# Pooling attention followed by a GELU MLP: K and V of a batch in one 128-partition tile, attention in full-array matmuls, and the remainder group second to last

## The chip, the cores and the metric

The kernel runs on one core of a Trainium2 chip. The metric is the device time of one execution in microseconds (us); each kernel was run four times or more, and medians are quoted. For each run the profile also gives the span (first to last instruction, some 2 us less than the timed value of the same run) and the mean clock that TensorE was granted, as a share of full speed.

The engines are called as in the profile: PE is TensorE, ACT is ScalarE, DVE is VectorE, POOL is GpSimd; SP issues DMAs, and "SPq" or "ACTq" lines are issues of DMAs by SP or ACT.

## The reference

```python
# q, k, v: (8 batches, 8 heads, 576 tokens, 64); w_in: 512 x 2048; w_out: 2048 x 512; all float32
def _attn_ref(q, k, v):
    ...
    k_p = k.reshape(B, H, Sp, pool, D).mean(axis=3)      # pool = 8, Sp = 72
    v_p = v.reshape(B, H, Sp, pool, D).mean(axis=3)
    scores = scale * np.matmul(q, k_p.transpose(0, 1, 3, 2))
    ...                                                   # softmax over the 72 pooled keys
    return np.matmul(attn, v_p)

def _moe_ref(x, w_in, w_out):                             # x: 4608 tokens x 512
    h = x @ w_in
    g = 0.5 * h * (1.0 + np.tanh(c * (h + 0.044715 * h * h * h)))
    return g @ w_out
```

The two matrix products of the MLP are nearly all of the work. Tokens are handled in nine groups of 512: groups 0 to 7 are the first 512 tokens of each batch, and the remainder group holds the last 64 tokens of all eight.

## The kernel before

Its main loop runs the MLP of one group and hangs pieces of the next group's attention into it at numbered steps. Steps 0 to 63 are the matmuls with W_in (64 of 128x512), steps 64 to 127 those with W_out. The MLP of one group, with what is hung into it, is called a stage below.

```python
    def scores(g, pr):                       # pr is a pair of heads
        ...
            for hh in range(2):
                p0 = 64 * hh                 # half of the array for each head
                nc.tensor.matmul(out=sc[:, hh, :], lhsT=kpT[p0:p0 + 64, g, pr, :],
                                 rhs=qT[p0:p0 + 64, pr, :], start=True, stop=True)
        ...
        nc.scalar.activation(out=e, in_=sc, func=ACT.Exp, scale=1.0 / 64.0)

    def attend(g, pr):
        ...                                  # den: sums of e, o: values, two half-array matmuls each
        nc.scalar.activation(out=lden, in_=den, func=ACT.Ln)
        nc.scalar.activation(out=r, in_=lden, func=ACT.Exp, scale=-1.0)
        ...
            nc.vector.tensor_tensor(out=xo, in0=o, in1=r, op=ALU.mult)
    ...
            p0, dp = (104, 6) if late else (64, 14)      # late: group 1, during group 0's MLP
            for pr in range(HP):
                at(p0 + dp * pr, scores, n, pr)
                at(p0 + dp * pr + dp // 2, attend, n, pr)
```

1/denominator is taken as exp(-ln(denominator)), so that exp and ln share one activation table; gelu needs another: in ACT's timeline in the prediction, exp, ln and exp (e, lden, r) follow each other without a table load, and one of 1.28 us stands between gelu and e. K and V are loaded with 72 partitions each and pooled by DVE in four trees a batch.

The softmax here doesn't subtract the row's maximum and nothing guards it: scores larger than these inputs give would overflow.

Of the kernel before, what the change touches and what calls it, by code (L numbers as in the profile page):

```python
# [8 lines left out]
F32 = mybir.dt.float32  # L9
BF16 = mybir.dt.bfloat16  # L10
# [7 lines left out]
def kernel(  # L18
# [12 lines left out]

    nc = tc.nc
# [6 lines left out]
    NG = B + 1  # L39
    MAIN = 512  # L40
    HP = H // 2

    consts = ctx.enter_context(tc.tile_pool(name="consts", bufs=1))
    wst = ctx.enter_context(tc.tile_pool(name="wst", bufs=2))
    kvp = ctx.enter_context(tc.tile_pool(name="kvp", bufs=6))
# [6 lines left out]
    kpT = consts.tile([128, B, HP, Sp], BF16, name="kpT")  # L52
    vs = consts.tile([Sp, B, H, D], BF16, name="vs")
    identb = consts.tile([128, 128], BF16, name="identb")
    ones8 = consts.tile([Sp, 64], BF16, name="ones8")

    st = [dict() for _ in range(NG)]


    def load_k(b, parts, eng):  # L60
        n = H // parts
        st[b]["k"] = []
        for i in range(parts):
            t = kvp.tile([Sp, n, 8, D], F32, name="kv")
            eng.dma_start(out=t, in_=k[b, i * n:(i + 1) * n].rearrange("h (sp pl) d -> sp h pl d", pl=8))
            st[b]["k"].append(t)

    def load_v(b, parts, eng):
        n = H // parts
        st[b]["v"] = []  # L70
        for i in range(parts):
            t = kvp.tile([Sp, n, 8, D], F32, name="kv")
            eng.dma_start(out=t, in_=v[b, i * n:(i + 1) * n].rearrange("h (sp pl) d -> sp h pl d", pl=8))
            st[b]["v"].append(t)

    def load_q(g, eng):
        t = work.tile([128, H, 4, D], F32, name="q_sb")
        st[g]["q"] = t
        if g < B:
            eng.dma_start(out=t, in_=q[g, :, :MAIN, :].rearrange("h (p j) d -> p h j d", j=4))  # L80
        else:
            for b in range(B):
                eng.dma_start(out=t[16 * b:16 * b + 16],
                              in_=q[b, :, MAIN:, :].rearrange("h (p j) d -> p h j d", j=4))


    def cast_q(g, js, eng):
        if "qb" not in st[g]:
            st[g]["qb"] = work.tile([128, 4, H, D], BF16, name="q_b")
        o = st[g]["qb"][:, js[0]:js[-1] + 1]  # L90
        i = st[g]["q"][:, :, js[0]:js[-1] + 1, :].rearrange("p h j d -> p j h d")
        if eng is nc.scalar:
            eng.copy(out=o, in_=i)
        else:
            eng.tensor_copy(out=o, in_=i)  # L95

    def pool8(t, res):
        nc.vector.tensor_tensor(out=t[:, :, 0:4, :], in0=t[:, :, 0:4, :], in1=t[:, :, 4:8, :], op=ALU.add)  # L98
        nc.vector.tensor_tensor(out=t[:, :, 0:2, :], in0=t[:, :, 0:2, :], in1=t[:, :, 2:4, :], op=ALU.add)  # L99
        nc.vector.tensor_tensor(out=res, in0=t[:, :, 0, :], in1=t[:, :, 1, :], op=ALU.add)  # L100

    def pool_k(b, i):
        if "kp" not in st[b]:
            st[b]["kp"] = work.tile([Sp, H, D], BF16, name="kp")
        t = st[b]["k"][i]
        n = t.shape[1]
        pool8(t, st[b]["kp"][:, i * n:(i + 1) * n, :])

    def pool_v(b, i):
        t = st[b]["v"][i]  # L110
        n = t.shape[1]
        pool8(t, vs[:, b, i * n:(i + 1) * n, :])

    def k_transpose(b, prs, eng):
        tp = psum.tile([128, HP, Sp], BF16, name="mm", tag="mm", bufs=4)
        for pr in prs:
            nc.tensor.transpose(out=tp[:, pr, :], in_=st[b]["kp"][:, 2 * pr:2 * pr + 2, :],  # L117
                                identity=identb[:Sp, :Sp])
        lo, hi = prs[0], prs[-1] + 1
        if eng is nc.scalar:  # L120
            eng.copy(out=kpT[:, b, lo:hi, :], in_=tp[:, lo:hi, :])
        else:
            eng.tensor_copy(out=kpT[:, b, lo:hi, :], in_=tp[:, lo:hi, :])  # L123

    def q_transpose(g, half):
        if "qT" not in st[g]:
            st[g]["qT"] = work.tile([128, HP, MAIN], BF16, name="qT")
        tp = psum.tile([128, 2, 4, 128], BF16, name="mm", tag="mm", bufs=4)
        for i in range(2):
            pr = 2 * half + i  # L130
            for j in range(4):
                nc.tensor.transpose(out=tp[:, i, j, :], in_=st[g]["qb"][:, j, 2 * pr:2 * pr + 2, :],  # L132
                                    identity=identb)
        nc.vector.tensor_copy(out=st[g]["qT"][:, 2 * half:2 * half + 2, :],  # L134
                              in_=tp.rearrange("p i j t -> p i (j t)"))

    def scores(g, pr):
        sc = psum.tile([Sp, 2, MAIN], F32, name="sc", bufs=1)
        qT = st[g]["qT"]
        if g < B:  # L140
            for hh in range(2):
                p0 = 64 * hh
                nc.tensor.matmul(out=sc[:, hh, :], lhsT=kpT[p0:p0 + 64, g, pr, :],  # L143
                                 rhs=qT[p0:p0 + 64, pr, :], start=True, stop=True)
        else:
            for b in range(B):
                for hh in range(2):
                    p0 = 64 * hh
                    nc.tensor.matmul(
                        out=sc[:, hh, 64 * b:64 * b + 64].rearrange("s (j p) -> s j p", j=4),  # L150
                        lhsT=kpT[p0:p0 + 64, b, pr, :],
                        rhs=qT[p0:p0 + 64, pr, :].rearrange("d (j b p) -> d b j p", j=4, b=B)[:, b],
                        start=True, stop=True)
# [4 lines left out]
    def attend(g, pr):  # L158
        e = st[g][("e", pr)]
        o = psum.tile([128, MAIN], F32, name="o", bufs=1)  # L160
        den = psum.tile([128, MAIN], F32, name="den", bufs=1)
        for hh in range(2):
            p0 = 64 * hh
            nc.tensor.matmul(out=den[p0:p0 + 64, :], lhsT=ones8, rhs=e[:, hh, :], start=True, stop=True)  # L164
        if g < B:
            for hh in range(2):
                p0 = 64 * hh
                nc.tensor.matmul(out=o[p0:p0 + 64, :], lhsT=vs[:, g, 2 * pr + hh, :],  # L168
                                 rhs=e[:, hh, :], start=True, stop=True)
        else:  # L170
            for b in range(B):
                for hh in range(2):
                    p0 = 64 * hh
                    nc.tensor.matmul(out=o[p0:p0 + 64, 64 * b:64 * b + 64], lhsT=vs[:, b, 2 * pr + hh, :],
                                     rhs=e[:, hh, 64 * b:64 * b + 64], start=True, stop=True)
        lden = work.tile([128, MAIN], F32, name="lden")
        nc.scalar.activation(out=lden, in_=den, func=ACT.Ln)  # L177
        r = work.tile([128, MAIN], F32, name="r")
        nc.scalar.activation(out=r, in_=lden, func=ACT.Exp, scale=-1.0)  # L179
# [3 lines left out]
        if g < B:  # L183
            nc.vector.tensor_tensor(out=xo, in0=o, in1=r, op=ALU.mult)  # L184
        else:
            nc.vector.tensor_tensor(out=xo.rearrange("d (j b p) -> d b j p", j=4, b=B),
                                    in0=o.rearrange("d (b j p) -> d b j p", j=4, b=B),
                                    in1=r.rearrange("d (b j p) -> d b j p", j=4, b=B), op=ALU.mult)


    def w_in_chunk(c):
        t = wst.tile([128, KO, 512], F32, name="wst")
        nc.sync.dma_start(out=t, in_=moe_w_in[:, 512 * c:512 * c + 512].rearrange("(ko p) f -> p ko f", p=128))
        return t

    def w_out_chunk(c):
        t = wst.tile([128, 4, DM], F32, name="wst")
        nc.sync.dma_start(out=t, in_=moe_w_out[512 * c:512 * c + 512, :].rearrange("(fo p) c -> p fo c", p=128))
        return t
# [11 lines left out]
    def mlp(g, hooks, pair_r):  # L211
# [11 lines left out]
        nc.scalar.preload_act_table_set(EXP_SET)  # L223
        nr = 2 if pair_r else 1
# [13 lines left out]
        for s in sorted(hooks):  # L238
            hook(s)
# [4 lines left out]
    load_k(0, 4, nc.sync)  # L244
    load_q(0, nc.scalar)
    nc.scalar.preload_act_table_set(EXP_SET)
    load_v(0, 2, nc.sync)
    make_identity(nc, identb)
    nc.gpsimd.memset(ones8, 8.0)
    wi = [w_in_chunk(0), w_in_chunk(1)]  # L250

    def cast_w(dst, t, eng, lo, hi):
        eng.tensor_copy(out=dst[:, lo:hi], in_=t[:, lo:hi])  # L253

    for pr in range(4):
        pool_k(0, pr)
        k_transpose(0, [pr], nc.scalar)
    cast_q(0, [0, 1], nc.scalar)
    cast_q(0, [2, 3], nc.gpsimd)
    q_transpose(0, 0)  # L260
    q_transpose(0, 1)
    pool_v(0, 0)
    pool_v(0, 1)
    scores(0, 0)
    for c in range(4):
        dst = w_in_b[:, :, 512 * c:512 * c + 512]
        if c < 3:
            scores(0, c + 1)
        attend(0, c)
        cast_w(dst, wi[c], nc.vector, 0, 2)  # L270
        cast_w(dst, wi[c], nc.gpsimd, 2, 4)
        if c < 2:
            wi.append(w_in_chunk(c + 2))
# [71 lines left out]
```

## Time and profile before

| | before |
|---|---|
| time, median (lowest to highest) | 356.21 us of 3 runs (353.85 to 356.89) |
| span of the profiled run, mean clock | 356.7 us, 0.983 (this run took 358.48 us, more than the three timed ones) |
| a middle stage | 34.2 us, of which PE 33.1 busy |
| group 0 until group 1's MLP | 79.6 us (its start, corrected for a short wait) |
| after the last W_out matmul | about 8 us, only stores |

The lines behind it are shown and read in the prediction. In a line of the timeline, the first number is the start, the second the time of the whole run of equal instructions (x7: seven), and brackets hold the idle time of the engine just before and what ended it. In a stretch view, each engine's busy us is followed by the number of its instructions; the last three columns are granted clock, DMA share and GB/s.

### The profile page before, as it was taken

Reading aid. Unit: us, or ns where it says so; the run is one execution under the profiler, and the core shown is the slowest. Engines: PE = TensorE matmul, PEld = TensorE weight load, DVE = VectorE, ACT = ScalarE, POOL = GpSimd, SP = SyncE. Lnnn points to the kernel's source line nnn. Section 1 sums busy time; section 2 is a strip of 40 time slices with the busy share of each in tenths; the row PEclk is TensorE's granted clock in tenths of the full one; section 3 lists DMA queues with packets and bytes.
Section 4 is the critical chain, followed back from the end, with each engine's and each line's share of the span. In section 5 each row is a group of like instructions: output and inputs, shape, how many; then the busy total and the mean of one; then the engine's idle time right before and its main releaser. Section 6 shows DMA issues by size and latency. Waiting matters only on the chain.

```text
span 356.7 us, 4161 instructions
## 1 busy us (share of the span) xinstructions
PE 309.4 (87%) x1656; PEld 132.1 (37%) x1656; DVE 141.5 (40%) x203; ACT 192.6 (54%) x276; POOL 30.9 (9%) x24
## 2 busy tenths in 40 slices
PE   0357974789899989998999899989988999899990
PEld 0212432224334533453345334433533354444440
DVE  2693133529333913590367137613861320230010
ACT  1265730286755675567556756675556657656500
POOL 0133432020200020002000200010020000000000
PEclk9999998899999999999999999999999999999997
DMA  7938999838701861185139314941610100010022
GB/s 236 250 136 324 290 349 230 230 106 211 229 33 59 231 182 59 60 238 146 59 99 255 89 62 125 237 111 59 125 24 29 59 31 0 31 61 29 2 58 60
DMA packets 28970, 46.40 MB, mean 130 GB/s; under 512 B 1816, under 2 KB 11032, under 8 KB 28952
## 3 DMA queue, kind: packets, MB, share of 16 engines
q1 hardware_dynamic: 27912, 45.10, 44.0%
q10 hardware_dynamic: 1040, 1.05, 1.0%
q8 instruction: 13, 0.21, 0.3%
q14 instruction: 5, 0.04, 0.0%
HBM read 36.70 MB, written 9.44 MB: 129 GB/s over the span
## 4 chain that ended last, share of the span: by engine, by line
PE 66%; DVE 12%; DMA 10%; ACT 8%; issue 1%; POOL 1%; SPq 0%; DVEq 0%
PE mm L232 30%; PE mm L220 26%; DMA kv<-in_v_dram 4%; DVE kv L98 4%; PE den L164 3%; ACT e L155 3%; DVE kv L99 3%; ACT L223 3%; DMA kv<-in_k_dram 2%; PE sc L143 2%; DMA wst<-in_moe_w_in_dram 2%; PE o L168 2%; PE mm L132 2%; DMA wst<-in_moe_w_out_dram 2%; DVE vs L100 1%; ACT gT L222 1%
## 5 line engine op out<-in xcount | busy, mean ns | idle before, releaser
L232 PE MATMUL mm<-w_out_b,gT 128*128 128x512 bf16 x576 | 138.4, 384 | 2.1 <-POOL w_out_b L253 2.0
L220 PE MATMUL mm<-xT,w_in_b 128*128 128x512 bf16 x576 | 131.4, 383 | 2.6 <-DVE xT L184 1.2
L222 ACT ACTIVATE gT<-mm 128x512 bf16<-128x512 f32 x144 | 86.0, 597 | 60.3 <-PE mm L220 60.2
L220 PEld LDWEIGHTS <-w_in_b 128*128 128x128 bf16 x576 | 55.7, 99 | 68.2 <-issue 6.6
L232 PEld LDWEIGHTS <-gT 128*128 128x128 bf16 x576 | 51.3, 98 | 74.0 <-issue 22.2
L155 ACT ACTIVATE e<-sc 72x1024 bf16<-72x1024 f32 x36 | 36.7, 1019 | 45.4 <-PE sc L143 42.2
L184 DVE TENSOR_TENSOR xT<-o,r 128x512 bf16<-128x512 f32 x32 | 22.1, 691 | 89.4 <-ACT r L179 82.4
L98 DVE TENSOR_TENSOR kv<-kv 72x1024 f32<-72x1024 f32 (+1 forms) x34 | 39.2, 1152 | 27.3 <-DMA kv<-in_k_dram 17.7
L236 DVE COPY osb<-mm 128x512 f32<-128x512 f32 x36 | 24.7, 690 | 60.4 <-PE mm L232 60.4
L177 ACT ACTIVATE lden<-den 128x512 f32<-128x512 f32 x36 | 21.4, 596 | 25.3 <-PE den L164 25.2
L95 POOL CAST q_b<-q_sb 128x2048 bf16<-128x2048 f32 (+1 forms) x9 | 16.4, 1818 | 203.7 <-DMA q_sb<-in_q_dram 142.7
L99 DVE TENSOR_TENSOR kv<-kv 72x512 f32<-72x512 f32 (+1 forms) x34 | 23.7, 698 | 1.2
L164 PE MATMUL den<-e,ones 72*64 72x512 bf16 x72 | 15.7, 428 | 9.1 <-ACT e L155 8.5
L179 ACT ACTIVATE r<-lden 128x512 f32<-128x512 f32 x36 | 22.7, 630 | 1.1
L132 PE MATMUL mm<-identb,q_b 128*128 128x128 bf16 x144 | 12.4, 238 | 6.2 <-POOL q_b L95 4.9
L168 PE MATMUL o<-e,vs 72*64 72x512 bf16 x64 | 13.8, 417 | 3.6 <-DVE xT L184 3.4
L143 PE MATMUL sc<-qT,kpT 64*72 64x512 bf16 x64 | 14.2, 439 | 3.0 <-DVE kpT L123 1.9
L134 DVE COPY qT<-mm 128x1024 bf16<-128x1024 bf16 x18 | 11.7, 681 | 8.3 <-PE mm L132 8.3
L132 PEld LDWEIGHTS <-q_b 128*128 128x128 bf16 x144 | 10.7, 108 | 10.6 <-POOL q_b L95 5.4
L164 PEld LDWEIGHTS <-ones 72*64 72x64 bf16 x72 | 5.3, 109 | 24.2 <-issue 24.1
L117 PE MATMUL mm<-identb,kp 72*128 72x72 bf16 x32 | 3.0, 201 | 12.7 <-DVE kp L100 12.7
L222 ACT ACT_TABLE_LOAD x9 | 11.5, 1283 | 0.2
(25 smaller groups left out, 70.4 us busy)
## 6 DMA issues: line engine op xcount, KB each, us to landing
kv<-in_v_dram SPq DMA_DIRECT2D x16, 576.0 KB
out_dram<-osb SPq DMA_DIRECT2D x32, 256.0 KB
kv<-in_k_dram SPq DMA_DIRECT2D x14, 576.0 KB
q_sb<-in_q_dram SPq DMA_DIRECT2D x7, 1024.0 KB
wst<-in_moe_w_in_dram SPq DMA_DIRECT2D x4, 1024.0 KB
wst<-in_moe_w_out_dram SPq DMA_DIRECT2D x4, 1024.0 KB
kv<-in_k_dram SPq DMA_DIRECT2D x4, 288.0 KB
q_sb<-in_q_dram ACTq DMA_DIRECT2D x1, 1024.0 KB
```

Of the source, the lines that this page charges most:

```text
L98: nc.vector.tensor_tensor(out=t[:, :, 0:4, :], in0=t[:, :, 0:4, :], in1=t[:, :, 4:8, :], op=ALU.add)
L99: nc.vector.tensor_tensor(out=t[:, :, 0:2, :], in0=t[:, :, 0:2, :], in1=t[:, :, 2:4, :], op=ALU.add)
L132: nc.tensor.transpose(out=tp[:, i, j, :], in_=st[g]["qb"][:, j, 2 * pr:2 * pr + 2, :], identity=identb)
L155: nc.scalar.activation(out=e, in_=sc, func=ACT.Exp, scale=1.0 / 64.0)
L164: nc.tensor.matmul(out=den[p0:p0 + 64, :], lhsT=ones8, rhs=e[:, hh, :], start=True, stop=True)
L177: nc.scalar.activation(out=lden, in_=den, func=ACT.Ln)
L179: nc.scalar.activation(out=r, in_=lden, func=ACT.Exp, scale=-1.0)
L184: nc.vector.tensor_tensor(out=xo, in0=o, in1=r, op=ALU.mult)
L220: nc.tensor.matmul(out=hp, lhsT=w_in_b[:, ko, fo * 128:(fo + 1) * 128], rhs=xT[:, ko, :], start=(ko == 0), stop=(ko == KO - 1))
L222: nc.scalar.activation(out=gT[:, fo, :], in_=hp, func=ACT.Gelu_apprx_tanh)
L232: nc.tensor.matmul(out=ops[i], lhsT=gT[:, fo, (r0 + i) * 128:(r0 + i + 1) * 128], rhs=w_out_b[:, fo, :], start=(fo == 0), stop=(fo == FO - 1))
L236: nc.vector.tensor_copy(out=osb, in_=ops[i])
```

## The change

The intent is to make PE's work whole. K and V of a batch share one tile of 128 partitions (64 each), so that one pooling tree does both; pooled V is moved into place by DMA. K is padded with zeros so that scores use the full array, and the values' tile holds 64 columns of 8.0 beside the 64 of V, so that one matmul for each head gives values in partitions 0 to 63 and sums in 64 to 127. The remainder group, whose stores are small, is handled before the last batch. The core of the diff:

```diff
+    R = B
+    seq = list(range(B - 1)) + [R, B - 1]
...
+    kpT = consts.tile([128, B, H, Sp], BF16, name="kpT")
+    vx = consts.tile([Sp, B, H, 2 * D], BF16, name="vx")
...
+    def pool(b, i0, i1):                       # one tree for K and V
+        ...
+    def move_v(b, engs):
+        for h in range(H):
+            p0 = 64 + h * Sp // NI
+            engs[h % len(engs)].dma_start(out=vx[:, b, h, 0:D], in_=st[b]["kvb"][p0:p0 + Sp // NI, :, 0, :])
...
+        for hh, o in ((0, X), (1, Y)):
+            if g < B:
+                nc.tensor.matmul(out=o, lhsT=vx[:, g, 2 * pr + hh, :], rhs=e[:, hh, :], start=True, stop=True)
...
+        nc.scalar.activation(out=lden[0:64], in_=X[64:128], func=ACT.Ln)
+        nc.scalar.activation(out=lden[64:128], in_=Y[64:128], func=ACT.Ln)
+        nc.scalar.activation(out=r, in_=lden, func=ACT.Exp, scale=-1.0)
+        for hh, o in ((0, X), (1, Y)):         # xo[half] = o[0:64] * r[half]
...
         # middle stages, where scores stood at 64 + 14 * pr and attend at 71 + 14 * pr:
+            at(62, scores, n, 0)
+            for pr in range(3):
+                at(78 + 12 * pr, scores, n, pr + 1)
+                at(78 + 12 * pr, attend, n, pr, False)
+            at(113, attend, n, 3, False)
...
         # during group 0's MLP, for group 1:
+            at(8, load_kv, n, k, 0, 0, NI, nc.sync)
+            at(20, load_kv, n, v, 64, 0, NI, nc.scalar)
+            at(24, load_q, n, 0, H, nc.sync)
+            at(25, w_out_load, 2)              # a load and its cast on POOL
+            at(26, w_out_load, 3)
+            at(27, cast_q, n, 0, H, nc.gpsimd)
+            at(64, pool, n, 0, NI)
+            at(64, move_v, n, [nc.sync])
+            at(84, q_transpose, n, 0, "sc", nc.vector)
...
+            at(40, loads, seq[n_ + 2])         # K, V and q of the group after the next
```

## The prediction

> **What bounds the kernel now.** I read the page first, then cut the span at the first W_in matmul (L220) of each group with the stretch view, then followed one middle stage on each engine in the timeline. The engines' line of the page:
>
> ```profile
> PE 309.4 (87%) x1656; PEld 132.1 (37%) x1656; DVE 141.5 (40%) x203; ACT 192.6 (54%) x276; POOL 30.9 (9%) x24
> ```
>
> PE is the bound on average, but an average hides four regimes. The stretch view (columns: PE, PEld, DVE, ACT, POOL busy us, clock, DMA share, GB/s):
>
> ```profile
> 0.00:28.00 28.00, 9.26 (x42) 3.77 (x43) 16.35 (x25) 10.60 (x17) 5.07 (x10) 1.00 0.72 215
> 29.00:46.00 17.00, 16.22 (x67) 6.81 (x66) 4.31 (x6) 10.30 (x17) 6.91 (x4) 1.00 0.94 294
> 46.00:79.00 33.00, 22.97 (x109) 8.90 (x107) 11.58 (x17) 10.36 (x14) 7.59 (x4) 0.90 0.81 235
> ...
> 148.60:182.80 34.20, 33.14 (x174) 14.01 (x173) 15.92 (x23) 21.10 (x30) 1.89 (x1) 1.00 0.47 132
> ...
> 348.60:356.70 8.10, 0.00 (x1) 0.00 (x0) 0.69 (x1) 0.00 (x0) 0.00 (x0) 0.68 0.24 59
> ```
>
> So: a start of 29 us that waits for loads; group 0's MLP, 50 us, with DMA at 0.8 to 0.94 of its time; seven stages of about 34.2 to 35.4 us in which PE is full; a last group of 27.8 us without attention; a tail of 8.1 us in which only stores run. In the first of them and in group 0 transfers decide, as this line of the PE timeline shows (the next group's q is cast late):
>
> ```profile
> 58.24 1.03 PE L132 MATMUL mm<-identb,q_b 128*128 128x128 bf16 x8 [4.91 <-POOL q_b L95]
> ```
>
> A middle stage, PE then ACT, from the last W_in matmul on:
>
> ```profile
> 163.53 0.41 PE L143 MATMUL sc<-qT,kpT 64*72 64x512 bf16 x2
> 163.87 1.69 PE L232 MATMUL mm<-w_out_b,gT 128*128 128x512 bf16 x7
> 166.61 0.41 PE L164 MATMUL den<-e,ones 72*64 72x512 bf16 x2 [1.06 <-ACT e L155]
> 166.83 0.41 PE L168 MATMUL o<-e,vs 72*64 72x512 bf16 x2
> 167.17 1.69 PE L232 MATMUL mm<-w_out_b,gT 128*128 128x512 bf16 x7
> 168.78 0.41 PE L143 MATMUL sc<-qT,kpT 64*72 64x512 bf16 x2
> ```
>
> ```profile
> 163.63 0.60 ACT L222 ACTIVATE gT<-mm 128x512 bf16<-128x512 f32 x1 [0.27 <-PE mm L220]
> 164.25 1.28 ACT L223 ACT_TABLE_LOAD   x1
> 165.54 1.02 ACT L155 ACTIVATE e<-sc 72x1024 bf16<-72x1024 f32 x1
> 167.06 0.60 ACT L177 ACTIVATE lden<-den 128x512 f32<-128x512 f32 x1 [0.49 <-PE den L164]
> 167.69 0.63 ACT L179 ACTIVATE r<-lden 128x512 f32<-128x512 f32 x1
> ```
>
> The only wait of the stage is 1.06 us: gelu 0.60, table load 1.28 and exp 1.02 stand between the last W_in matmul and the first denominator. A W_in matmul is issued every 0.216 us (24 of them take 5.18 in the chain). A half-array pair costs 0.34 (163.53 to 163.87) against 0.43 for two whole ones, but the seven matmuls after each take 1.61 and not 1.51. The stage adds up: 128 x 0.216 = 27.65, transposes 1.03, four times scores 0.34 + denominators and values 0.56 = 3.6, the wait 1.06, eight times 0.105 after half-array pairs = 0.84; 34.2.
>
> [...]
>
> **The change, part by part.**
>
> *Middle stages.* Removed: the half-array pairs[...] (3.6 + 0.84) and the wait of 1.06. Added: 16 whole matmuls, 16 x 0.216 = 3.46, and about 0.5 more for nine K transposes instead of four. Without new waits the stage would be 27.65 + 0.9 + 0.6 + 3.46 = 32.6, a gain of 1.6. But the instruction order of the changed kernel shows what is new on ACT: scores of the first pair stand before the last gelu, so exp comes between gelu 15 and 16 with a table load on each side: exp table, e0, gelu table, gelu, exp table. Two more loads a stage, 2.56 us. Each pair also has two Ln of 64x512 (0.60 each; the time follows the elements per partition, not the partitions) where it had one, and two DVE multiplies (0.69 each). X and Y have one buffer each, and both hold sums and values, so both are freed only by the multiplies at the chain's end; before, the denominators were freed by Ln.
>
> From the first W_out matmul = 0: gelu 15 ends at -0.45; table 0.83, e0 1.86, table 3.15, gelu 3.76 (needed at 4.1: just in time), table 5.05. PE issues scores 1 at 3.03 and X0, Y0 until 3.89. ACT: e1 until 6.10, Ln 6.7, Ln 7.3, r 7.95; DVE multiplies until 8.67 and 9.39. PE reaches X1 at 3.89 + 12 x 0.216 + 0.43 = 6.9, gets it at 8.72 and Y1 at 9.44: stalls of 1.8 and 0.5. Then e2 9.0, Ln X1 9.76, Ln Y1 10.48, r 11.13, multiplies 11.85 and 12.57; X2 is reached at 12.7: no stall. e3 13.9, Ln 14.5 and 15.1, r 15.75, multiplies 16.47 and 17.19; X3 is reached at 13.12 + 11 x 0.216 = 15.5: stalls of 1.0 and 0.5. Sum 3.8 us. The stage: 32.6 + 3.8 = **36.4 against 34.2**, 2.2 worse. DVE has less to do in pooling (2304, 1152 and 576 elements at about 1.02 ns plus 0.17, and a copy, 5.0 us against four times 2.3), but it bounds nothing there.
>
> *Start.* q, K and V are 3.4 MB; at 290 GB/s they land near 13.5, and w_in (4.2 MB at 320, the rate of 26.8 to 53.5 in this trace) by 26.6. Pooling and transposes are through near 17, scores at 17.3. V then has to move by DMA: half of the moves are issued by SP behind w_in, so the first values come near 28.5 and the remaining chain (three exp, three Ln and r, the last multiply: about 7 us) ends near 36, against 31 now. It is later, yet hidden: q of group 1 is cast on POOL after the last w_out cast. Behind w_in come 7.6 MB: 26.6 + 23.8 = 50.4, cast 52.3, q cast 54.2. The transposes at step 84 are reached at 36 + 18.1 = 54.1 anyway.
>
> *Rest of group 0.* SP issues the loads of group 2 (3.4 MB, 10.7 us) before it moves V of group 1: 50.4 + 10.7 + about 1.7 = 62.8, and X0, otherwise reached near 60.7, waits for it. From X0 the same recurrence with 8 matmuls between gives 13.7 us to the last multiply, 76.5, and the osb copy that frees a bank stands behind it on DVE: the next group starts at **77.2**. Now it starts effectively at 79.6 (80.28 less three matmuls). Gain 2.4.
>
> *Remainder second to last.* Its scores and values become 64-column matmuls, 128 in all, that no longer run two at a time: 0.06 each (as the transposes: 0.45 for 8) where pairs took 0.40 and 0.68; with smaller stalls that stage is near 37.9. The stage that hosts group 7 has no K transposes: 35.8. The tail changes for the better. Now each quarter of the last group needs eight stores:
>
> ```profile
> 339.00 15.45 SPq L209 DMA_DIRECT2D out_dram<-osb  x32
> ```
>
> The last is issued at 354.0, 4.7 us after its data, and the program ends 2.7 later. One store of 256 KB: 0.7 for the copy, 2.7, and 0.75 for the larger transfer: 4.15 against 8.1. Gain 3.9.
>
> *Sum.* 77.2 + 5 x 36.4 + 37.9 + 35.8 + 27.8 + 4.15 = 364.9. The stalls are added as if none overlapped with slack in the semaphores, and the author's steps may have been set from runs, so I take 362.
>
> **The rivals.** (1) *The stalls at X and Y do not come*, and PE stays the bound: 32.6 per stage, 7 x 3.8 = 27 less, about 338. For it: ACT is only 54% busy. Against it: idle shares say nothing of a serial chain, and the chain's durations are all measured. Half of the stalls gone would be 349 to 351. (2) *Loads decide the first 80 us more than I think*: [...]V's moves behind 3.4 MB at 290 GB/s, put the next group at 82 and the sum at 369. For it: DMA share 0.94. (3) *V's moves overtake the loads*[...]: the first MLP starts at 29, but q's cast at 54 holds it, and only the 2 us before X0 are saved: 360.
>
> **Range and chances.** The stage's loss is counted seven times, so an error of 1 us in it is 7 in the sum; the start adds 4. Range 350 to 371. Faster by 2% means under 349, for which half of the stalls must be wrong: 0.13. Slower by 2% is over 363.3: 0.42. Within: 0.45.
>
> **What would show it.** Right: middle stages of 36 to 37 us; PE waits before the X matmul of the second pair of about 1.8 us and of the fourth of about 1.0, released by DVE xT; 33 table loads instead of 19; the last store under 4.5 us after the last matmul; the first Y matmul waiting for the vx copy until near 28. Wrong: middle stages of 33 us with no wait on xT (rival 1); the first group's values on time (rival 3); a remainder stage under 35.

The forecast's sum came to 364.9 us, and to 362 after the 3 us taken off it. The table load of 1.28 us is read from ACT's timeline (164.25, the exp at 165.54), and the 0.105 us after a half-array pair, eight of which are the 0.84, from PE's (1.61 us from the start of seven matmuls to what follows them, and not 1.51). That V's copies wait behind the loads which SP issued before them, on which the 28.5 and the 62.8 rest, the trace of before does not show; later runs do (X0 waits 3.99 us for them in the fourth experiment, and not in the fifth, where they are issued first). The 1.7 us for the copies in the 62.8 is an estimate of mine without a line behind it. The 290 GB/s is near the 294 of the stretch from 29 to 46, and 0.75 us for 256 KB is an estimate from the 349 GB/s in the page's highest slice. That ACT's time follows the elements per partition is seen after the change: 0.594 us for an Ln of 64x512, 0.596 for one of 128x512.

## The result, and the profile after

| | before | after |
|---|---|---|
| time, median of 4 (lowest to highest) | 355.59 us (353.85 to 356.89) | **384.49 us** (383.88 to 385.38) |
| ratio | | 1.0818, interval 1.0761 to 1.0874 |
| span, mean clock | 356.7 us, 0.983 | 383.1 us, 0.960 |

The profiled run of before took 358.48 us, 2.9 above its median, so differences of spans against it come out some 2 to 3 us larger than those of the timed medians. A ratio here is the mean time of one kernel's fast runs over the mean time of the other's fast runs of the same rounds, so it is not quite the ratio of the medians quoted. The change is slower, by 8%, and outside the predicted range.

The engines' line of the page of the kernel after:

```profile
PE 320.2 (84%) x1632; PEld 144.6 (38%) x1632; DVE 139.5 (36%) x178; ACT 229.6 (60%) x319; POOL 42.2 (11%) x25
```

PE has 24 instructions fewer than before, yet is busy for 11 us more and idle for 16 us more. Both need a cause. The stretch view of the kernel after, cut like that of before: the start, group 0 until the q of group 1 is there, two middle stages, the tail.

```profile
0.00:33.07 33.07, 11.67 (x49) 4.11 (x50) 13.80 (x19) 11.77 (x15) 17.60 (x14) 1.00 0.90 299
33.07:61.87 28.80, 21.17 (x86) 8.79 (x85) 10.28 (x5) 12.16 (x19) 11.37 (x4) 0.95 1.04 255
...
164.12:200.67 36.55, 33.10 (x170) 15.17 (x169) 15.43 (x20) 26.04 (x36) 1.90 (x1) 1.00 0.48 125
200.67:238.90 38.23, 34.78 (x170) 15.60 (x169) 15.42 (x20) 26.03 (x36) 1.90 (x1) 0.96 0.46 119
379.00:383.10 4.10, 0.00 (x0) 0.00 (x0) 0.69 (x1) 0.00 (x0) 0.00 (x0) 1.00 0.17 64
```

The two middle stages do the same work with the same instructions. The first, at full clock, takes 36.55 us, as predicted. The second takes 1.68 us more, all of it in PE's busy time, and its clock is 0.96. The tail has gone from 8.1 to 4.1 us, as predicted. Group 0 lasts to 85.61, not to 77.2.

**A stage on ACT.** The timeline of ACT in the stage from 85.61 to 125.89, the first events after the last but one gelu:

```profile
102.79 1.28 ACT L158 ACT_TABLE_LOAD   x1
104.08 1.02 ACT L158 ACTIVATE e<-sc 72x1024 bf16<-72x1024 f32 x1
105.12 1.28 ACT L222 ACT_TABLE_LOAD   x1
106.42 0.60 ACT L222 ACTIVATE gT<-mm 128x512 bf16<-128x512 f32 x1
107.03 1.28 ACT L224 ACT_TABLE_LOAD   x1
108.33 1.02 ACT L158 ACTIVATE e<-sc 72x1024 bf16<-72x1024 f32 x1
```

The early exp before the last gelu costs two more table loads, 2.56 us, in which ACT does nothing for the chain (from the end of the exp at 105.10 to the start of the gelu at 106.42 it is 1.32 us, table load included); the second pair's exp ends at 109.35, and everything behind it is late.

**The same stage on PE**, and the two lines of the stage from 164 that stand for the same places:

```profile
107.16 2.75 PE L232 MATMUL mm<-w_out_b,gT 128*128 128x512 bf16 x12
...
112.01 0.38 PE L184 MATMUL X<-e,vx 72*128 72x512 bf16 x1 [1.67 <-DVE xT L199]
112.82 0.38 PE L184 MATMUL Y<-e,vx 72*128 72x512 bf16 x1 [0.43 <-DVE xT L199]
113.04 4.44 PE L232 MATMUL mm<-w_out_b,gT 128*128 128x512 bf16 x12
...
121.63 0.38 PE L184 MATMUL X<-e,vx 72*128 72x512 bf16 x1 [0.92 <-DVE xT L199]
...
188.48 0.38 PE L184 MATMUL X<-e,vx 72*128 72x512 bf16 x1 [1.67 <-DVE xT L199]
...
189.50 2.75 PE L232 MATMUL mm<-w_out_b,gT 128*128 128x512 bf16 x12
```

The waits are the predicted ones: 1.67 and 0.43 before X and Y of the second pair, 0.92 and 0.43 before those of the fourth, all released by the multiply xT. But the twelve matmuls after the first two waits take 4.44 us at 113.04 and 2.75 at 107.16 and 189.50. The stretch view of 6.8 microseconds in each of the two stages, cut in halves, shows why:

```profile
110.26:113.67 3.41, 1.31 (x6) 0.42 (x5) 2.06 (x3) 3.00 (x5) 0.00 (x0) 1.00 0.98 301
113.67:117.08 3.41, 3.41 (x9) 1.20 (x8) 2.06 (x3) 0.79 (x2) 1.90 (x1) 0.50 0.23 86
185.35:188.76 3.41, 1.74 (x8) 0.62 (x6) 0.99 (x2) 3.30 (x5) 0.00 (x0) 1.00 0.82 162
188.76:192.17 3.41, 2.98 (x15) 1.39 (x15) 2.22 (x4) 1.82 (x3) 0.00 (x0) 1.00 1.02 343
```

After the waits the granted clock is 0.50 in the one stage and 1.00 in the other: nine matmuls run in the second line and fifteen in the fourth, though PE also waits 0.43 us there. The loss of 1.69 us (4.44 less 2.75) is that of about 3.4 us at half speed. It comes in five of the seven stages, in those that start at 85.61, 125.89, 200.67, 238.90 and 313.57. Twice elsewhere PE also starts slowly after idling. This costs 2.05 us at the start of group 1 (24 matmuls in 7.39 us and not 5.34) and 2.7 in group 0's first 64 (16.69 and not 13.98). The second of these is not new: the first matmuls of group 0 come 0.43 us apart in the kernel before too. The clock column reads 1.00 there, but the trace has no record of the clock before 38.59 us here and before 34.09 in the kernel before.

The sixteen records of the clock in this trace all begin whole multiples of 3.41 us apart (59.07, 65.90, 82.96, 89.79, 113.68, 117.09 and so on); the points at these distances are called marks here. PE was not idle for the whole of such a stretch: waits of 1.67 and 0.43 us, with one matmul between them, were enough.

The same marks show where the stage from 164 differs, which is spared with the same waits. The four lines above are cut at them. In the stage from 85 both waits fall between two marks, where PE is busy for 1.31 us of 3.41, and the half clock begins at the next mark. In the stage from 164 the mark at 188.76 stands between the two waits. In the five stages that are hit, PE idles 1.9 to 2.1 us between the two marks around its waits; in the stage from 164 it idles 1.67. The run of the fourth experiment below has the same waits in its middle stages: two of its seven are hit, those from 161.26 and 236.02 (2.1 us between two marks), and in the others no such stretch is idle for more than 1.68. In the middle stages of these two runs, where a stage lies against the marks thus went with whether its waits cost 1.7 us more. This is no general threshold: at the end of group 0 of the first experiment (78.77 to 82.18), 1.57 us of idle time were followed by the half clock (24 matmuls in 7.30 us and not 5.34), and in the kernel before, 1.71 us between two marks (47.75 to 51.16) left it at 1.00.

**Group 0.** The timelines of PE, DVE and POOL of the kernel after, where the q of group 1 is awaited:

```profile
61.87 1.03 PE L136 MATMUL tp<-identb,q_b 128*128 128x128 bf16 x8 [7.59 <-POOL q_b L90]
```

```profile
54.77 2.93 DVE L98 TENSOR_TENSOR kv<-kv 128x1152 f32<-128x1152 f32 x1
57.73 2.33 DVE L100 TENSOR_TENSOR kvb<-kv 128x576 bf16<-128x576 f32 x1
```

```profile
52.35 7.11 POOL L286 CAST w_out_b<-wst 128x2048 bf16<-128x2048 f32 x2 [15.58 <-DMA wst<-in_moe_w_out_dram]
59.40 2.41 POOL L90 CAST q_b<-q_sb 128x2048 bf16<-128x2048 f32 x1
```

Two casts of W_out take 7.11 us, though one takes 1.9 alone (four casts of the same shape in this kernel, at 17.95 to 27.37). The adds beside them take 2.93 and 2.33, though an add of the same shape takes 1.36 and 0.76 where POOL is quiet (shown with the sixth experiment). Each engine is slow beside the other: each of these instructions starts while one of the other engine is under way and is longer than alone, the second add by 1.57 us, the third by 1.57, the two casts by 3.3 together, the q cast by 0.52. By what mechanism, the trace does not show. The prediction had none of it.

### The profile page after: what moved, and what is told of

Same layout as the page of the kernel before. It is cut to its first block, busy times and chain, and to the rows that moved or that the text cites. A ratio compares the mean times of both kernels' runs of the same rounds, so it can differ in the third digit from the quotient of the medians.

```text
span 383.1 us, 4260 instructions
## 1 busy us (share of the span) xinstructions
PE 320.2 (84%) x1632; PEld 144.6 (38%) x1632; DVE 139.5 (36%) x178; ACT 229.6 (60%) x319; POOL 42.2 (11%) x25
## 4 chain that ended last, share of the span: by engine, by line
PE 51%; ACT 21%; DMA 11%; issue 6%; DVE 5%; POOL 3%; ACTq 1%; DVEq 0%
PE mm L220 28%; PE mm L232 18%; DMA wst<-in_moe_w_out_dram 7%; ACT e L158 6%; DVE xT L199 4%; DMA kv<-in_v_dram 3%; ACT r L191 3%; ACT lden L190 3%; ACT L222 2%; ACT L158 2%; ACT lden L189 2%; POOL w_out_b L286 2%; ACT gT L222 2%; PE tp L136 2%; PE Y L184 2%
## 5 line engine op out<-in xcount | busy, mean ns | idle before, releaser
L199 DVE TENSOR_TENSOR xT<-X,r 64x512 bf16<-64x512 f32 x32 | 21.8, 683 | 151.6 <-ACT r L191 151.6
L90 POOL CAST q_b<-q_sb 128x2048 bf16<-128x2048 f32 x8 | 15.7, 1961 | 221.3 <-DMA q_sb<-in_q_dram 180.0
L97 DVE TENSOR_TENSOR kv<-kv 128x2304 f32<-128x2304 f32 (+1 forms) x10 | 20.8, 2079 | 19.7 <-DMA kv<-in_v_dram 19.5
L136 PE MATMUL tp<-identb,q_b 128*128 128x128 bf16 x144 | 12.5, 240 | 16.9 <-DVE q_b L90 9.3
L189 ACT ACTIVATE lden<-X 64x512 f32<-64x512 f32 x32 | 19.0, 594 | 11.9 <-PE X L184 10.1
L184 PE MATMUL X<-e,vx 72*128 72x512 bf16 x28 | 10.6, 378 | 17.3 <-DVE xT L199 17.3
L150 PE MATMUL sc<-qT,kpT 128*72 128x512 bf16 x64 | 20.9, 410 | 3.0 <-ACT e L158 2.3
L199 DVE TENSOR_TENSOR xT<-Y,r 64x512 bf16<-64x512 f32 x32 | 21.9, 684 | 1.0
L190 ACT ACTIVATE lden<-Y 64x512 f32<-64x512 f32 x32 | 19.0, 593 | 2.9 <-PE Y L184 2.2
L184 PE MATMUL Y<-e,vx 72*128 72x512 bf16 x28 | 10.9, 388 | 6.3 <-DVE xT L199 6.3
L142 DVE COPY qT<-tp 128x1024 bf16<-128x1024 bf16 x16 | 10.9, 684 | 14.1 <-PE tp L136 14.1
```

What stands on the lines that cost most here:

```text
L136: nc.tensor.transpose(out=tp[:, i, j, :], in_=st[g]["qb"][:, j, 2 * pr:2 * pr + 2, :], identity=identb)
L150: nc.tensor.matmul(out=sc[:, hh, :], lhsT=kpT[:, g, h, :], rhs=qT, start=True, stop=True)
L184: nc.tensor.matmul(out=o, lhsT=vx[:, g, 2 * pr + hh, :], rhs=e[:, hh, :], start=True, stop=True)
L189: nc.scalar.activation(out=lden[0:64], in_=X[64:128], func=ACT.Ln)
L190: nc.scalar.activation(out=lden[64:128], in_=Y[64:128], func=ACT.Ln)
L199: nc.vector.tensor_tensor(out=a, in0=in0, in1=in1, op=ALU.mult)
```

## The experiments

Runs 1 to 4, 5 to 8 and 9 to 12 were each made on one chip and share their runs of the kernel before; the thirteenth was made alone. All outputs were correct.

| run | time, median | ratio to before [interval] | span, clock |
|---|---|---|---|
| e1_steps14 | 356.42 | 1.0019 [0.9975, 1.0064] | 354.8, 0.981 |
| e2_scores64 | 366.55 | 1.0298 [1.0255, 1.0342] | 365.2, 0.981 |
| e3_filler | 376.46 | 1.0577 [1.0530, 1.0625] | 374.2, 0.979 |
| e4_qcast_first | 382.58 | 1.0782 [1.0713, 1.0851] | 378.6, 0.967 |
| e5_v_before_loads | 351.74 | 0.9872 [0.9816, 0.9927] | 349.8, 0.985 |
| e6_casts_on_act | 348.54 | 0.9779 [0.9711, 0.9847] | 346.8, 0.990 |
| e7_rem_last | 360.90 | 1.0125 [1.0063, 1.0188] | 358.6, 0.980 |
| e8_apart | 361.54 | 1.0145 [1.0084, 1.0206] | 359.5, 0.980 |
| e9_order | 342.94 | 0.9644 [0.9594, 0.9694] | 341.2, 0.998 |
| e10_order_start | 347.55 | 0.9766 [0.9720, 0.9813] | 346.1, 0.989 |
| e11_order_steps13 | 343.13 | 0.9641 [0.9595, 0.9687] | 341.6, 0.990 |
| e12_before_rem | 353.87 | 0.9948 [0.9890, 1.0005] | 351.8, 0.989 |
| e13_order_steps13 | **338.90** | **0.9532** [0.9471, 0.9593] | 336.9, 1.000 |

**My theory** after the result: the stage's waits are made by the steps at which scores and attention are hung in, not by the full-array matmuls; the waits in turn bring the half clock; and group 0 is late by its order of transfers and casts. **The rivals:** the merged matmuls, with their sums held until the multiply, are what costs; the half clock has nothing to do with the waits; group 0 is late because loads into 64 partitions are slow (a guess that no run isolates).

### 1. The steps of before in the changed kernel (e1_steps14)

```diff
-            at(62, scores, n, 0)
-            for pr in range(3):
-                at(78 + 12 * pr, scores, n, pr + 1)
-                at(78 + 12 * pr, attend, n, pr, False)
-            at(113, attend, n, 3, False)
+            for pr in range(HP):
+                at(64 + 14 * pr, scores, n, pr)
+                at(71 + 14 * pr, attend, n, pr, False)
```

> The changed kernel with one edit: in the middle stages the steps of the kernel before (scores of a pair at 64+14p, its sums and values at 71+14p) instead of 62/78/90/102/113. Theory A (the loss of a stage is the chain through the single X and Y, and the low clock follows from those waits): first scores stand behind the last gelu, so 19 table loads; a wait of 1.0 us for the first exp as in the kernel before; no wait on xT, as X is reached 0.1 us after its multiply; no stretch at half clock after 100 us. Stage 27.65 + 0.9 + 0.6 + 3.46 + 1.0 = 33.6, against 36.6 (or 38.2 with a low clock); total 385 less 7 x 3 less 5 x 1.7 = 355. Rival B (the stage is long because whole-array matmuls or pooling in one tree cost more): stages stay over 35.5. Rival C (the low clock comes from the matmuls, not from waits): stretches at half clock stay.

Measured: 356.42 us, and a stage of 33.70. The steps alone are worth 28 us: some 19.3 for the waits and table loads of the seven stages (2.85 in each of the first five, 36.55 less 33.70, and 2.4 and 2.7 in the last two) and about 8.5 for five half clocks. PE in a middle stage of this run:

```profile
139.01 0.38 PE L184 MATMUL X<-e,vx 72*128 72x512 bf16 x1 [1.07 <-ACT e L158]
...
139.44 1.68 PE L232 MATMUL mm<-w_out_b,gT 128*128 128x512 bf16 x7
```

No wait on xT is left. What is left, 1.07 us for the exp, is what the kernel before had in the same place (1.06), and no half clock follows. So with its old steps the change is as fast as before, and no faster: its stages win 0.5 us each (34.2 less 33.7, 3.5 in all) and its tail 3.9, and group 0 gives 5.4 back (85.0 against 79.6), which leaves 2 of gain between the spans of the two profiled runs and none in the timed ones (the profiled run of before was a long one).

### 2. Only the first scores back to step 64 (e2_scores64)

```diff
-            at(62, scores, n, 0)
+            at(64, scores, n, 0)
```

> The changed kernel with one edit: the first scores of a middle stage at step 64 instead of 62, behind the last gelu, so two table loads fewer a stage (19 in all). Theory A, worked as in the prediction: second pair waits 0.3 for X1 (was 1.67) and 0.5 for Y1; fourth pair still 0.95 and 0.5; stage 34.9 against 36.6; no half clock after the second pair, as the wait is 0.8 in all. Total about 385 - 7 x 1.7 - 8.5 = 364. If the table loads did not sit on the chain: stage unchanged at 36.6, only the low clock might go.

Measured: 366.55 us, a stage of 35.14, with waits of 0.26 and 0.43 before pair 2 and of 0.91 and 0.43 before pair 4, and no half clock. The early exp with its two table loads thus costs 1.4 us of a stage directly, and the half clock besides. The waits before pair 4 are those of the steps 78 + 12 and 113; the first experiment removed them too.

### 3. More work instead of the wait (e3_filler)

Eight extra matmuls, whose result nobody reads, stand before X of the second pair, where PE waits.

```diff
+        if pr == 1 and n_ > 0:
+            fill = psum.tile([128, MAIN], F32, name="mm", tag="mm", bufs=4)
+            for i in range(8):
+                nc.tensor.matmul(out=fill, lhsT=identb, rhs=gT[:, i, :], start=True, stop=True)
         for hh, o in ((0, X), (1, Y)):
```

> The changed kernel with eight matmuls more in front of the X matmul of the second pair of each stage (8 x 0.216 = 1.73 us into a spare bank, read by nobody), where PE stands idle for 1.67 now. If the half clock of about 3.4 us after this pair comes from the idle time in front of it, it is gone in all stages, stages are 36.5 to 36.7, and the total falls by some 8 us to 376, though PE does more work. If it comes from anything else[...], the half clock stays in five of seven stages and the total is 385 or more. The waits of the fourth pair (0.92 and 0.43) stay.

Measured: 376.46 us, faster by 8 us (span: 8.9) than the changed kernel, although PE has 56 matmuls more to do. A middle stage on PE:

```profile
146.12 1.89 PE L185 MATMUL mm<-gT,identb 128*128 128x512 bf16 x8
147.95 0.38 PE L188 MATMUL X<-e,vx 72*128 72x512 bf16 x1
...
148.97 2.75 PE L236 MATMUL mm<-w_out_b,gT 128*128 128x512 bf16 x12
```

X is not a moment sooner (the chain on ACT and DVE is as it was), the stage is 36.54 us, and no middle stage falls to half clock. Idle PE time brought the half clock; filling it took it away. This shows the cause of the 8.5 us; the rival, a clock that falls for another reason, would have been unmoved or worse. Nor is it luck in where the stages lie: between two marks of the clock no middle stage of this run has more than 1.34 us of idle PE time.

### 4. q cast before the W_out casts (e4_qcast_first)

```diff
-            at(25, w_out_load, 2)
-            at(26, w_out_load, 3)
-            at(27, cast_q, n, 0, H, nc.gpsimd)
+            at(25, cast_q, n, 0, H, nc.gpsimd)
+            at(26, w_out_load, 2)
+            at(27, w_out_load, 3)
```

> The changed kernel with the cast of group 1's q on POOL before the casts of the third and fourth quarter of w_out instead of behind them. Theory: q is there near 45, so the wait of 7.6 us before the transposes at step 84 goes; the transposes come near 54. K's transposes then wait for the pooling, which runs beside the two w_out casts and ends near 60 to 62 as now, so scores start near 62 instead of 67.8 and the second group's MLP near 80 instead of 85.6; total about 379. Rival (the copies of V behind the loads of group 2 hold the first X instead): scores come early but X0 stays near 68 to 70, and nothing is gained; then the V copies of the trace end near 68.

Measured: 382.58 us (380.42 to 385.59; the profiled run is the fastest), the second group at 85.49 against 85.61. The transposes of q come at 52.74, 9 us sooner and without a wait, and nothing is won: K's transposes then wait 3.65 us for the pooling, and the first values wait for V. PE of this run:

```profile
68.53 0.61 PE L184 MATMUL X<-e,vx 72*128 72x512 bf16 x1 [3.99 <-DMA vx<-kvb]
```

V's copies are issued by SP behind the 3.4 MB of the loads of group 2. This is the wait that the prediction named ("X0 ... waits for it"), which the late q had hidden in the changed kernel: one wait took the place of another.

### 5. q first, and V's copies before the loads (e5_v_before_loads)

On top of the first and the fourth experiment's edits:

```diff
-            at(40, loads, seq[n_ + 2])
+            at(65 if n_ == 0 else 40, loads, seq[n_ + 2])
```

> The kernel of the first experiment (steps 64+14p and 71+14p in the middle stages), with group 1's q cast before the casts of w_out's third and fourth quarter, and with the copies of group 1's V issued before group 2's loads instead of behind them. In the run with the q cast alone X0 then waited 4.0 us for those copies, at 68.5. Theory: the copies were late because they stood behind 3.4 MB of loads on one queue; now X0 comes near 64.4 and the second group's MLP near 80 instead of 85; total 356.4 - 5 = 351.5. If the copies are late for another reason (their issue, a semaphore), X0 stays near 68 and the total near 356.

Measured: 351.74 us. X0 comes at 64.39 and the second group at 80.03, 5 us sooner than in the first experiment. The two waits of group 0 stood behind each other: the q cast alone gave nothing (fourth experiment), both cures together 5 us. V's copies alone were moved in no run; the changed kernel's X0 has no wait for them that they could have removed.

### 6. Two casts on ACT (e6_casts_on_act)

On top of the fifth: the last two casts of W_out are made by ACT at steps 66 and 67.

```diff
+            at(66, w_out_cast, 2)          # nc.scalar.copy in place of nc.gpsimd.tensor_copy
+            at(67, w_out_cast, 3)
```

> The same, and the casts of w_out's third and fourth quarter on ACT (idle there, behind the last gelu of group 0) instead of POOL. Theory: the POOL casts (3.65 us instead of 1.89) and the pooling adds of group 1 on DVE (128x1152 in 2.93 us instead of 1.36, 128x576 in 2.33 instead of 0.77) slowed each other down; apart, the adds take 2.56, 1.36 and 0.77, pooling ends near 56 instead of 59, and the second group's MLP starts near 76; total 347.5. If the adds were slow because of loads that wrote SBUF then, they stay at 2.9 and 2.3 and nothing moves against the run before.

Measured: 348.54 us, the second group at 76.40. DVE's adds without POOL beside them:

```profile
54.19 1.36 DVE L98 TENSOR_TENSOR kv<-kv 128x1152 f32<-128x1152 f32 x1
55.58 0.76 DVE L100 TENSOR_TENSOR kvb<-kv 128x576 bf16<-128x576 f32 x1
```

2.93 and 2.33 became 1.36 and 0.76, and K's transposes wait 0.52 us and not 3.73. POOL and DVE slowing each other was worth 3.2 us here (351.74 less 348.54).

### 7. The remainder last again (e7_rem_last)

On top of the first experiment:

```diff
-    seq = list(range(B - 1)) + [R, B - 1]
+    seq = list(range(B)) + [R]
```

(with the batch indices that follow from it).

> The kernel of the first experiment with the remainder group last, as in the kernel before the change. The prediction's term: a tail of 8.1 us instead of 4.2, all else equal: 356.4 + 3.9 = 360.3. If the order also matters elsewhere (the stage that hosts the remainder loses its pooling), up to 0.5 off.

Measured: 360.90 us, a ratio of 1.0125 against the first experiment's 1.0019: about 3.8 us worse. The last copy stands at 349.91 and the span ends at 358.55, 8.6 us later. In the changed kernel the order of the groups did all that was expected of it; the twelfth experiment shows less of it in the kernel before.

### 8. Sums and values apart again (e8_apart)

On top of the first experiment, the middle stages of whole batches take sums and values in half-array pairs (the branch that the changed kernel keeps for group 0):

```diff
-                at(71 + 14 * pr, attend, n, pr, False)
+                at(71 + 14 * pr, attend, n, pr, n < B)
```

> The kernel of the first experiment with sums and values apart in the middle stages (half-array pairs, one Ln, one multiply, as in group 0), scores in whole arrays. Theory: with no wait on X and Y the whole-array form saves what the prediction worked out for values and sums: 4 x (0.34 + 0.22 + 0.10) = 2.64 against 4 x 0.43 = 1.73, so the stage is 33.7 + 0.9 = 34.6, in six stages; total 356.4 + 5.4 = 361.8. ACT is busy 0.6 x 4 less a stage and DVE 0.7 x 4 less, which moves nothing.

Measured: 361.54 us and a stage of 34.49, against 33.70: 0.79 us for each of the six stages with a whole batch, 4.7 us. The merged matmuls are worth having, with the right steps. The rival, that they are what cost, falls.

### 9. Group 0 rearranged (e9_order)

On top of the sixth experiment: V of group 1 is loaded right behind K by SP, pooling and V's copies move to the first half of group 0's MLP, and the transposes, scores and attention of group 1 come earlier in the second.

```diff
+            at(8, load_kv, n, v, 64, 0, NI, nc.sync)
+            at(9, load_q, n, 0, H, nc.sync)
+            at(10, cast_q, n, 0, H, nc.gpsimd)
+            at(12, w_out_load, 2)
+            at(13, w_out_load, 3)
+            at(14, pool, n, 0, NI)
+            at(15, move_v, n, [nc.sync])
+            at(66, w_out_cast, 2)
+            at(71, w_out_cast, 3)
+            ...                            # transposes at 64, 66, 68
+                at(70 + 12 * pr, scores, n, pr)
+                at(76 + 12 * pr, attend, n, pr, False)
```

> The kernel of the sixth experiment (middle steps of 14, V before the loads of group 2, w_out casts on ACT) with group 0 rearranged: V of group 1 issued right behind K and ahead of w_out's second half, its pooling and V copies in the first half of group 0's MLP, transposes at steps 64, 66, 68, scores from step 70 and sums from 76, 12 apart. Theory: what held group 0 was the order of its transfers, not the amount; q, K and V are ready before step 64 at 49, so the second half takes 64 x 0.216 + 0.9 + 0.4 + 3.5 = 18.6 plus about 1.5 of waits, and the second group's MLP starts near 69.5 instead of 76.4. Total 348.5 - 7 = 341.5. If the bytes decide instead (w_out's second half comes later now), w_out is missing at step 96 or 112 and the gain is under 3 us.

Measured: 342.94 us, the second group at 72.42, later than the 69.5 expected. This beats both kernels. The mean clock is 0.998. A q cast that ends 3.04 us late is what is left.

### 10. V's copies before the second half of W_in (e10_order_start)

On top of the ninth. The first values wait 2.02 us for V's copies at 25.77 in the changed kernel, as SP issues its share of them behind all of W_in (from 17.98 on; the cast of W_in's last quarter starts at 25.47). Here they stand before its second half:

```diff
-        for i in range(2):
+        for i in range(2 if c == 0 else 0):
...
-    move_v(0, [nc.sync, nc.scalar])
+    move_v(0, [nc.sync])
+    for i in range(2):
+        nc.sync.dma_start(out=w_in_s[1][:, :, 512 * i:512 * i + 512], in_=...)
```

> The same, with the copies of group 0's V all issued by SP and ahead of the second half of w_in, where now half of them stand behind it and the others hold ACT before the first exp. In the changed kernel Y waited 2.0 us for such a copy and the first exp 1.4 us behind ACT's issues. Theory: the first MLP starts near 30.5 instead of 33, the second group's near 67.5; total 339.5. If the loads then hold the second half of group 0, the total stays near 341.5.

Measured: 347.55 us, 4.6 worse than the ninth; a clear miss. The first MLP did start sooner, at 30.34 against 32.73. But SP issued the copies only when the pooled V was there, at 17.69, and what stands behind them in the program waited with them; and all eight copies of 9 KB are now issued by SP, which took 6.04 us, some 0.75 for each. SP and then POOL of this run:

```profile
17.69 6.04 SPq L106 DMA_DIRECT2D vx<-kvb  x8
23.77 0.99 SPq L274 DMA_DIRECT2D w_in_s<-in_moe_w_in_dram  x2
```

```profile
29.02 1.89 POOL L285 CAST w_in_b<-w_in_s 128x2048 bf16<-128x2048 f32 x1 [6.60 <-DMA w_in_s<-in_moe_w_in_dram]
```

W_in's second half was issued at 23.77 and not at 15.07 as in the ninth experiment: 2.6 us of this are the wait for the pooled V, until 17.69, and 6.0 the issuing of the eight copies. Fewer bytes moved meanwhile (127 GB/s in the page's slice from 17.3 to 26.0, between 296 and 394), and the cast that stood at 22.43 in the ninth experiment stands at 29.02. Every later load is late by as much; q of group 1 is awaited for 7.94 us, and the second group starts at 77.37. I had counted the copy's place among SP's issues, and neither the time at which SP can issue it nor the time that issuing takes.

### 11. Steps thirteen apart (e11_order_steps13)

On top of the tenth, the middle stages' scores stand at 64, 80, 93 and 106 and attention at 74, 87, 100 and 113, so that the first exp and its table load have ten W_out matmuls to hide behind instead of seven.

```diff
-                at(64 + 14 * pr, scores, n, pr)
-                at(71 + 14 * pr, attend, n, pr, False)
+                at(64 if pr == 0 else 67 + 13 * pr, scores, n, pr)
+                at(74 + 13 * pr, attend, n, pr, False)
```

> The same as the run before it, with middle steps of 13: first scores at 64, later ones at 80, 93, 106, sums and values at 74, 87, 100, 113. The one wait left in a middle stage is 1.07 us for the first exp at step 71; three steps later it is 0.4. A distance of 13 matmuls and four whole ones is 3.67 us, the chain from X to its free buffer 3.05 plus what the next exp takes of it, so no wait on X or Y. Stage 33.7 - 0.65 = 33.05; total 339.5 - 4.5 = 335. If the chain is tighter than worked out, waits of up to 0.9 a pair on xT come back and the total is 340 or more.

Measured: 343.13 us, 4.4 better than the tenth, and a stage of 33.05, both as expected (the 335 in the text was reckoned from a tenth experiment that was not yet known to have missed). The wait for the exp is 0.43 and not 1.07.

### 12. The kernel before with only its groups reordered (e12_before_rem)

```diff
+    seq = list(range(B - 1)) + [B, B - 1]
+    for n_ in range(NG):
+        g = seq[n_]
```

(with the indices that follow).

> The kernel before the change with the remainder group second to last and nothing else. The tail falls from 8.1 us to 4.2 as in the changed kernel; all stages as before. Total 356.3 - 3.9 = 352.4, 0.989 of the kernel before. If the eight small stores of a quarter were not what makes the tail, it stays at 356.

Measured: 353.87 us, 0.9948 of before, with an interval that just reaches 1. The span fell from 356.7 to 351.8 (against the long profiled run of before), and from the last copy (347.76) to the end it is 4.0 us, as expected; the timed gain is about 2 us, less than the 3.8 that the seventh experiment lost by the reverse. The tail is thus shown in the trace of both; that its gain in time is less here is not settled, as the runs of before beside this one alone lie between 353.9 and 358.0.

### 13. Both cures together (e13_order_steps13)

The ninth experiment (its start untouched) with the steps of the eleventh.

> This is e9 (group 0 rearranged, the start as in the changed kernel) with the middle stages' steps of e11 (scores at 64, 80, 93, 106; attention at 74, 87, 100, 113). Theory: the two sources of loss, group 0's loads and the waits of the middle stages, are independent terms of one sum, and e10's miss came from its start alone (the second half of w_in issued behind the V copies). Then the seven stages go from about 33.7 to 33.05 us and the whole is e9's 342.9 less e11's gain of 4.4 over e10: about 338.5 us. Rival: e11 gained only because e10 had left something to gain (a later start with other waits), and the steps are worth little where group 0 is in order: 341 to 343 us with stages of 33.5 or more.

Measured: 338.90 us, 0.9532 of before and, by the two ratios to before, 0.9884 of the ninth. A middle stage of this run in the stretch view, and PE's one wait in the stage before it:

```profile
139.68:172.73 33.05, 32.47 (x168) 15.29 (x169) 15.42 (x21) 23.45 (x34) 1.89 (x1) 1.00 0.53 138
```

```profile
124.99 0.38 PE L184 MATMUL X<-e,vx 72*128 72x512 bf16 x1 [0.43 <-ACT e L158]
```

The two terms add, so they are independent, and the tenth experiment's miss was its start alone. This is the best version found: 16.9 us under the kernel before in the timed medians. Between the two profiled spans it is 19.8, of which 7.0 are group 0 (72.6 against 79.6), 3.9 the tail, and the rest, about 9, the stages.

## Why the prediction was wrong

The waits that it named were found at each place. Its sum was 18 us short because two terms were missing, the clock after idle PE time and the slowing of POOL and DVE beside each other, and 3 more were taken off it without a reason from the trace. Its terms against the trace of the kernel after (span 383.1):

| term | predicted | measured | difference |
|---|---|---|---|
| second group's MLP starts | 77.2 | 85.61 | +8.4 |
| five middle stages | 182.0 | 191.41 | +9.4 |
| the stage beside the remainder's attention | 37.9 | 36.55 | -1.3 |
| the stage beside group 7's | 35.8 | 37.62 | +1.8 |
| last group | 27.8 | 27.8 | 0 |
| tail | 4.15 | 4.1 | 0 |
| sum | 364.9 | 383.1 | +18.2 |

**Middle stages: "1.8 and 0.5", "1.0 and 0.5", "36.4 against 34.2".** Right where the clock holds: 1.67 and 0.43, 0.92 and 0.43, 36.55. Experiments 1 and 2 show that the step numbers cause them. The 32.6 for a stage without waits was right too: 33.70 less the wait of 1.07 in the first experiment, 33.05 less 0.43 in the thirteenth, are 32.6 each.

**The missing term: the clock.** The prediction took 0.216 us for a matmul throughout; at half clock it is 0.43. Five times a stage lost 1.7 us after its waits, 8.5 in all (6.8 in the five stages, 1.7 in the one beside group 7's), and group 1's start 2.05. Experiment 3 shows that idle PE time is the cause. The trace of before had a hint that I passed over: its waits of 1.06 us left the clock at 1.00, and only group 0, with waits of several us, stood at 0.90, while the first matmuls of group 0 came 0.43 us apart.

**The missing term: group 0, "50.4, cast 52.3, q cast 54.2".** The cast of q ended at 61.81. Of these 7.6 us, about 1.95 are POOL's wait for a load of W_out until 52.35, where the prediction had the last one landed at 50.4; 1.9 are a second W_out cast that was still to be done then; 3.85 are what the casts took longer beside DVE's adds (7.11 less 3.78, and 2.41 less 1.89). Experiment 6 shows the other side of this: without casts beside them the adds took 1.36 and 0.76 us and not 2.93 and 2.33. About 1.2 us more lie behind X0: from there to the next group it is 15.6 us (69.97 to 85.61) and not 14.4. I had counted POOL's casts as if nothing ran beside them, with the pooling of the same group hung in at the very time. "Before X0" was right as a mechanism: V's copies do stand behind group 2's loads, and experiment 4 shows 3.99 us of it; in the changed kernel the late q hid it.

**"It is later, yet hidden" (the start).** The first MLP started at 33.07 and not 36, by which that estimate was 3 us too long, and it was indeed hidden: what held the second group was the chain from the loads.

**The remainder.** Its matmuls of 64 columns were cheaper than the 0.06 each that I took (eight of X at 296.33 and eight of Y at 296.56: 0.03 each), so the stage was 36.55 and not 37.9. The tail was right to 0.05 us, and experiment 7 shows its worth.

**"So I take 362".** The 3 us taken off for slack had no line behind them, and the trace shows no slack: the waits came in full in all stages. That the range ended at 371 was this error too: both terms left out could only add.

**The rivals of the prediction.** The first (no stalls) fell. The second (loads decide the first 80 us) was nearest, with 82 and 369 us, but part of its reason has no run behind it; what the experiments show is the order of casts and copies (5 us in the fifth), and the slowing of POOL and DVE beside each other (3.2 us in the sixth). Whether loads into 64 partitions are slow was not isolated: the kernel after moved 255 GB/s from 33 to 62 with the DMA engines busy throughout, and no run changed only that. The third fell with experiments 4 and 5: V's copy came late behind the loads, and in time before them.

## What to carry to other kernels

In these runs a wait in the bounding engine cost more than its length where the clock fell after it: waits of 1.67 and 0.43 us cost 1.7 us more in five of seven stages. Waits of 1.07 us (first experiment) or of 0.91 and 0.43 (second) brought no half clock. So add that term to a change which makes PE idle, and look at the granted clock in short stretches (0.50 for 3.41 us here) and not only at the mean (0.960). Where a change rearranges the data and the schedule together, try the new data with the old schedule first: here the new matmuls were worth 4.7 us, and the new steps cost 28. When one late transfer is cured, look for the one behind it: in group 0 the cure of one gave nothing and the cure of both 5 us. In the tenth experiment the load behind V's copies was issued 8.7 us later: 2.6 were the copies' wait for their data at the issuing engine, and 6.0 the issuing of eight copies of 9 KB.
